# Attention and two MLPs on one core: the first MLP of blocks one to five from float32r to float16 parts

## The chip, the cores and the metric

The kernel runs on one core of a Trainium2 chip. The metric is the device time of one execution in microseconds. A profiled execution gives the span from the first instruction to the last, and the busy times of TensorE (PE, with its weight loads as PEld), VectorE (DVE), ScalarE (ACT), GpSimd (POOL) and the queue that issues DMAs (SP).

## The reference

q, k and v have 4 batches, 8 heads, 576 positions and 64 dimensions; there are 2304 tokens of width 512 and two MLPs with 2048 inner columns, all float32.

```python
scores = scale * np.matmul(q, k.transpose(0, 1, 3, 2))
scores = np.where(block_i >= block_j, scores, -1000000000.0)   # blocks of 64 positions
attn = np.exp(scores - np.max(scores, axis=-1, keepdims=True))
attn = attn / (np.sum(attn, axis=-1, keepdims=True) + 1e-09)
x = np.matmul(attn, v)          # then heads side by side: 2304 x 512
h = x @ moe_w_in
x = np.maximum(0.01 * h, h) @ moe_w_out
h = x @ moe2_w_in
return (h * (1.0 / (1.0 + np.exp(-h)))) @ moe2_w_out
```

## The kernel before

The tokens are worked in six blocks of 384. Attention of block b+1 runs beside the first MLP of block b; the second MLP follows for all tokens at the end, in seven products for each pair (a Strassen scheme).

The weights lie in memory as pairs of 32-bit words (64-bit numbers): `convert` makes float32 of them. `w0`, the sign and the top word of each number are taken from the raw load: ACT scales the top word (L429), ACT or DVE puts the low word's bits in place (L437 to L443), DVE masks the sign (L446), shifts the exponent by 3 (L450, `shifted`) and adds the two (L455, `added`). With `joint` the last two are one instruction, shift and or (L459, `joined`); the second MLP's weights have that form. The first MLP's w1 comes in 32 pieces of 128x512, two for each of 16 inner chunks f (side 0 of the input weight, side 1 of the output weight). Block zero uses them whole in float32, as they arrive.

For blocks one to five each operand is a float32r pair, high and low part, and each product three matmuls (low weight by high x, high by low, high by high). `split_weights` makes w1's parts (high on ACT or DVE at L381 and L383, low on DVE at L392), `take_pair` those of x from PSUM (L1089, L1094), and `g_hi`, `g_lo` those of the gate. `first_layer` (L1611 to L1613) and `second_layer` (L1640) are the matmuls: 4 chunks of 128 rows by 3, 12 each, so 24 of 384 columns in a step (blk, f), 16 steps a block. They are issued in two cuts of six.

Attention of a block has four groups of two heads. For each, `values_of` loads V, takes its largest absolute value (L1023), spreads it and turns it over the partitions by a transposing DMA (L1029), reduces again (L1034), forms a power of two and its inverse from the exponent (L1037 to L1048), and splits V in float16 parts (L1052, L1057). Scores (L1305) are float32r parts, the weights of attention float16 parts, turned by transposing DMAs; `weigh_all` issues their products with V (L1155) into one bank, and `take_pair` scales them back as it takes x out. One staging ring of V holds a single group. x has two sets of tiles, for even and odd blocks: x of block b+1 waits until the first layers of block b-1 are through (`x_free`).

The order of the instructions on every engine is computed before: `Schedule` takes tasks with dependencies, durations and ranks and plays them through; among what is ready the lowest rank goes first. A step's rank is 16 times its block plus f; `GATE`, `SHORT` and `CHAIN` put gates, attention on PE and the maximum of a row ahead of all. The first MLP's and the second's matmuls form one chain (`in_turn`): first layer of a step, then second layer of the step before. Attention of block b has ranks from 16(b-1) + `ATT` on, over 12.8 (`ATT_SLOPE` 0.8 of 16); splits of w1 for step f have 16 + f + 55; conversions 10.5 + 0.7 f.

`SLOTS` divides 32 slots of two 128x512 float32 tiles: w1's parts of chunk f are in slots 2f and 2f+1, the whole w1 in the last 15 to 16 until block zero has used it, and as slots become free in block five the second MLP's operands go there (`emptied`, `place_of`). After the last step of a block four evacuations take its output to staging tiles and memory (`add_second`, `evac`); the second layer of the next block's first step waits for all four, since it uses the same banks.

Of the kernel before, what the change touches and what calls it, by code (L numbers as in the profile page):

```python
# [19 lines left out]
P = 128  # L20
# [13 lines left out]
NATIVE = 15  # L34
# [11 lines left out]
ATT0, ATT1, ATT, ATT_SLOPE, AHEAD, V_LATE = 11.0, 0.3, 60.0, 0.8, 7.5, 0.0  # L46
# [15 lines left out]
SQUARE, RANGE = 2.0**-16, 2.0**-68  # L62

# [178 lines left out]
def attn_mlp_mlp(  # L242
# [56 lines left out]
    SLOTS = {"y": (0, 3), "x": (3, 3), "e": (6, 3), "xw": (9, 2), "t1": (11, 1), "t2": (12, 1), "l": (30, 2)}  # L299
# [24 lines left out]
    def emptied(name):  # L324

        return [steps[base + slot_of(name)[-1] // 2].t_g2]
# [83 lines left out]
    def convert(src, f, sl, rk, load_rank, to=None, slow=0, lag=0, joint=False, free=()):  # L410
# [41 lines left out]
        def added(e):  # L452
            ci = d["c"].bitcast(I32)
            d["x"] = d["c"].bitcast(F32) if to is None else to
            engine[e].tensor_tensor(d["x"].bitcast(I32), d["y"].bitcast(I32), ci, op=ALU.add)  # L455
# [35 lines left out]
    def first_weights():  # L491

        got = []
        for i in range(2 * NF):
            f, sl = i // 2, slice((i % 2) * DM, (i % 2 + 1) * DM)
            rk = CONV0 + CONV1 * f
            to = wx[f][:, sl] if f < NATIVE else None
            got.append(convert(w1, f, sl, rk, LOAD0 + RAW0 + 20 * i if i < 4 else rk - CONV_LOAD, to, slow=LATER if i < 4 else 0))
        return got

    def split_weights():
# [3 lines left out]
        for i in range(2 * NF):  # L505
            f, sl = i // 2, slice((i % 2) * DM, (i % 2 + 1) * DM)
            d, t_x, users = w1_got[i]
# [6 lines left out]
            deps = [t_x]  # L514
            for at in (2 * f, 2 * f + 1):
                j = at - len(spare) - len(kq1)
                if at in slot_of("xw"):
                    deps += [t for u in units for t in (u.t_turn, u.t_pv)]
                elif at < len(spare):
                    deps += x_done[0]  # L520
                elif j < 0:
                    deps += kq1_users
# [24 lines left out]
    def second_places():  # L547
# [8 lines left out]
        place.step = slot_of("xw")[-1] // 2  # L556
        w2_places.append((place, 2 * TWO))
        k = slot_of("t2")[-1] + 1
        while len(w2_places) < 7 * NF // 2 - 2:
            place = Place(lambda t, k=k: slot(k, "r" if t == F32R else "rh", t), ())  # L560
            place.step = k // 2
            w2_places.extend([(place, 0), (place, DM)])
            k += 1
# [4 lines left out]
    def place_of(p, k, halved=False):  # L568
# [7 lines left out]
        if hasattr(place, "step"):  # L576
            deps = y_there[NBLK - 2][:2] if place.step is None else [steps[base + place.step].t_g2]
# [285 lines left out]
    v_ring, vp_ring = ring("v", VR, F32), ring("vp", 2 * VR, F16)  # L863
    v_small = pp.tile([P, 8], F32, tag="vs", name="vs")
# [19 lines left out]
    class Group:  # L884


        def __init__(self):
            self.x, self.evac = None, []
            self.t_turn, self.t_top, self.v_users = None, None, []

    heads, groups, s_users, units = [], [], [], []
# [4 lines left out]
    t_least = plan.add(  # L896
# [3 lines left out]
    def attention(blk):  # L900
# [95 lines left out]
        def values_of(mine, rk):  # L996
            g, k = groups[-1], len(groups) % 2
            last, older = (groups[-2] if len(groups) > 1 else None), (groups[-3] if len(groups) > 2 else None)
            total = sum(words_of_v(two[0][3]) for two in mine)
            g.rs, g.rv = v_ring.take(total), vp_ring.take(2 * total)  # L1000
            stage, both = v_ring.view(g.rs, total), vp_ring.view(g.rv, 2 * total)
            hi, lo = both[:, :total], both[:, total:]
            small = v_small[:, 4 * k : 4 * k + 4]
            most, top, mult, g.back = (small[:, i : i + 1] for i in range(4))
            t_load, g.v, at = [], [], 0
            for two in mine:
                _, b, _, q1, h = two[0]
                nj, n = (q1 + P - 1) // P, words_of_v(q1)

                def load(b=b, h=h, nj=nj, to=stage[:, at : at + n]):  # L1010
                    nc.sync.dma_start(
                        out=to.rearrange("p (h x) -> p h x", h=2),
                        in_=vL[b, h : h + 2, :, :nj, :].rearrange("h p j d -> p h (j d)"),
                    )

                t_load.append(dma(freed(g.rs), rk + 0.5, P * 4 * n, load, lag=V_LAG))
                for i in (0, 1):
                    sl = slice(at + i * n // 2, at + (i + 1) * n // 2)
                    g.v.append([part[:, sl].rearrange("p (j d) -> p j d", d=D) for part in (hi, lo)])
                at += n  # L1020

            def summed(e):
                nc.vector.tensor_reduce(most, stage, axis=AX.X, op=ALU.max, apply_absolute_value=True)  # L1023
# [1236 lines left out]
```

## Time and profile before

| | |
|---|---|
| median of 3 runs | 898.11 us (897.71 to 899.44) |
| profiled execution | 897.39 us, span 895.7 us |
| PE busy | 882.3 us (99%), 6569 matmuls |
| PEld busy | 796.9 us (89%) |
| DVE busy | 775.9 us (87%), 1794 instructions |
| ACT busy | 626.8 us (70%), 1428 instructions |
| granted TensorE clock | 1.000 over the span |
| HBM read and written | 93.85 and 35.65 MB |

Matmuls are pipelined and their ends are modelled, so a busy PE is not PE at its peak; the pitch at which matmuls start says more. Block zero's MLP runs from about 35 to 136 us, block one from 132, block five to 548; the two halves of the second MLP follow. A row of a timeline gives the start, the duration, the engine, the line and operation, and what the instruction writes and reads by the program's names (h, l: parts of x; the w and slot names: weights; s: scores; vs: V's scalars).

### The profile page before, as it was taken

To read this page: it belongs to the slowest core of one execution; us is meant where nothing else is said; L and a number is where in the kernel's file an instruction comes from. 1 tells how busy PE (TensorE), PEld (TensorE's weight loads), DVE (VectorE), ACT (ScalarE), POOL (GpSimd) and SP (SyncE) were. 2 spreads that over 40 slices of the span, in tenths; PEclk is the share of its full clock that TensorE was granted. 3 is DMA by queue.
4 is the path that set the end of the run, shared out by engine and by line. 5 is a ranking of instruction groups with operands and counts; after the bars stand their busy time and mean duration, and the time that the engine had idled before them with its cause. 6 is when DMAs were issued, how large, how long until landed. Compare 5 with 4: busy or idle time off the path is not lost.

```text
span 895.7 us, 18467 instructions
## 1 busy us (share of the span) xinstructions
PE 882.3 (99%) x6569; PEld 796.9 (89%) x6569; DVE 775.9 (87%) x1794; ACT 626.8 (70%) x1428; POOL 17.8 (2%) x81
## 2 busy tenths in 40 slices
PE   9999999999999999999999999999999999999997
PEld 4655569999999999999999998999999988888886
DVE  6898899998889899888755998889887999999986
ACT  7998688776766677777645766979887995444432
POOL 0000000000000000000000000000000000000000
PEclk9999999999999999999999999999999999999999
DMA  7588836766675688866625446687865884554531
GB/s 240 173 234 199 237 110 167 141 144 148 155 156 121 144 187 156 157 170 156 126 45 177 153 159 194 221 289 226 292 229 191 296 263 135 166 152 132 166 106 59
DMA packets 181291, 156.13 MB, mean 174 GB/s; under 512 B 110416, under 2 KB 157264, under 8 KB 181200
## 3 DMA queue, kind: packets, MB, share of 16 engines
q1 hardware_dynamic: 181200, 154.97, 63.4%
q8 instruction: 51, 0.84, 0.4%
q14 instruction: 40, 0.33, 0.1%
HBM read 93.85 MB, written 35.65 MB: 145 GB/s over the span
## 4 chain that ended last, share of the span: by engine, by line
PE 81%; DVE 11%; ACT 4%; DMA 2%; issue 2%; SPq 0%; DVEq 0%; ACTq 0%
PE acc L1640 11%; PE acc L2055 8%; PE s L2055 5%; PE h L1611 5%; PE h L1612 5%; PE h L1613 5%; PE s L1305 4%; PE u L1640 4%; PE h L1606 4%; PE x L1155 3%; PE u L2055 3%; PE x L2055 2%; PE acc L1876 2%; PE acc L1877 2%; PE acc L1632 2%; PE acc L1878 2%
## 5 line engine op out<-in xcount | busy, mean ns | idle before, releaser
L1323 ACT ACTIVATE p<-s,st 128x288 f32<-128x288 f32 (+4 forms) x120 | 62.5, 522 | 46.3 <-DVE st L1315 26.9
L1668 ACT ACTIVATE g<-h 128x384 f32<-128x384 f32 x96 | 46.8, 488 | 49.5 <-PE h L1613 43.2
L1305 PE MATMUL s<-k,q 128*128 128x288 f32 (+5 forms) x288 | 65.8, 324 | 1.2 <-ACT p L1323 1.0
L1640 PE MATMUL acc<-ghi,w 128*128 128x384 f32 x255 | 66.6, 337 | 0.0
L1337 ACT ACTIVATE hl<-p,st 128x576 f16<-128x576 f32 (+5 forms) x91 | 54.9, 622 | 14.1 <-DVE st L1333 5.4
L392 DVE TENSOR_TENSOR glo<-g,ghi 128x384 fp32r<-128x384 f32 x80 | 44.3, 553 | 20.4 <-ACT ghi L381 19.9
L1342 DVE SCALAR_TENSOR_TENSOR hl<-p,st,hl 128x576 f16<-128x576 f32 (+4 forms) x96 | 59.0, 625 | 2.3 <-ACT hl L1337 1.5
L1611 PE MATMUL h<-h,w 128*128 128x384 f32 x180 | 60.7, 337 | 0.0
L2055 PEld LDWEIGHTS <-y 128*128 128x128 f16 x525 | 51.2, 98 | 6.8 <-issue 0.8
L1305 PEld LDWEIGHTS s<-k,q 128*128 128x128 f32 x288 | 47.5, 188 | 7.2 <-ACT p L1323 2.9
L1613 PE MATMUL h<-h,w 128*128 128x384 f32 x160 | 53.6, 335 | 0.0
L1612 PE MATMUL h<-l,w 128*128 128x384 f32 x160 | 53.6, 335 | 0.0
L2055 PEld LDWEIGHTS <-x 128*128 128x128 f16 x492 | 48.1, 98 | 6.0 <-issue 0.5
L1928 ACT ACTIVATE e<-e 128x384 f32<-128x384 f32 (+1 forms) x72 | 42.4, 622 | 9.0 <-DVE e L1908 8.7
L429 ACT ACTIVATE cy<-raw 128x512 f32<-128x512 f32 x64 | 42.8, 669 | 8.3 <-DMA raw<-w 3.9
L1937 ACT ACTIVATE h<-e 128x384 f32<-128x384 f32 x96 | 46.8, 488 | 1.7
L1640 PEld LDWEIGHTS acc<-ghi,w 128*128 128x128 f32 x255 | 45.5, 188 | 0.8
L1640 PE MATMUL acc<-glo,w 128*128 128x384 f32 x120 | 40.2, 335 | 0.0
L381 ACT ACTIVATE ghi<-g 128x384 fp32r<-128x384 f32 x75 | 39.1, 522 | 1.2
L1315 DVE TENSOR_REDUCE st<-s 128x1 f32<-128x320 f32 (+3 forms) x72 | 36.4, 505 | 2.2
L1155 PEld LDWEIGHTS <-vp 128*64 128x64 f16 x1296 | 31.5, 111 | 7.4 <-issue 7.3
L1876 PE MATMUL acc<-h,w 128*128 128x384 f32 x96 | 32.3, 337 | 1.7 <-ACT l L381 1.5
(374 smaller groups left out, 2756.9 us busy)
## 6 DMA issues: line engine op xcount, KB each, us to landing
raw<-w SPq DMA_DIRECT2D x64, 512.0 KB, 4.8
raw<-g SPq DMA_DIRECT2D x64, 256.0 KB, 3.3
g<-e SPq DMA_DIRECT2D x48, 192.0 KB, 3.5
g<-e SPq DMA_DIRECT2D x24, 384.0 KB, 3.4
kqr<-kq_l SPq DMA_DIRECT2D x16, 480.0 KB, 3.9
kqr<-kq_l SPq DMA_DIRECT2D x16, 416.0 KB, 3.8
v<-vL SPq DMA_DIRECT2D x16, 320.0 KB, 3.2
y<-yT SPq DMA_DIRECT2D x12, 384.0 KB, 3.7
```

The lines of the kernel that those rows point to most:

```text
L1155: nc.tensor.matmul(o[i * D : (i + 1) * D, c], v[i][part][:, j], p[i][a], start=start and t == 0, stop=stop and t == len(terms) - 1,)
L1305: nc.tensor.matmul(s[:, :w], hd.q[:, a : a + P], hd.k[:, k0:k1], start=i + j == 0, stop=i == len(hds) - 1 and j == 1,)
L1323: nc.scalar.activation(p[:rows, k0:k1], u.s[piece][:rows, :w], AF.Exp, bias=nm[:rows], accum_out=s2[:rows, piece : piece + 1])
L1337: nc.scalar.activation(hl[:rows, 0, :n], p[:rows], AF.Copy, scale=rc[:rows])
L1342: nc.vector.scalar_tensor_tensor(hl[:rows, 1, :n], p[:rows], rc[:rows], hl[:rows, 0, :n], op0=ALU.mult, op1=ALU.subtract)
L1611: nc.tensor.matmul(h, w1_lo[s.f][:, sl], hi[:, c, : s.n], start=c == 0, stop=False)
L1612: nc.tensor.matmul(h, w1_hi[s.f][:, sl], lo[:, c, : s.n], start=False, stop=False)
L1613: nc.tensor.matmul(h, w1_hi[s.f][:, sl], hi[:, c, : s.n], start=False, stop=c == NC - 1)
L1640: nc.tensor.matmul(s.acc[c][:, : s.n], a, b, start=s.f == 0 and i == 0, stop=s.f == NF - 1 and i == 2)
L1668: nc.scalar.activation(s.g, s.h[:, :n], AF.Prelu, alpha=LEAK)
L1876: nc.tensor.matmul(o, wlo[:, w], xhi[:, x], start=k == 0, stop=False)
L2055: nc.tensor.matmul(o, a[:, x], b, start=i == 0 and j == 0 and q == 0, stop=i == NP - 1 and q == 2, skip_group_check=True,)
```

## The change

Blocks one to five of the first MLP work with float16 parts instead of float32r ones. So that the parts lie in float16's range, both operands are scaled by powers of two. For V there is one factor for a block instead of one for a group: `values_of_all` loads all four groups at once into staging places of their own, takes four maxima and their maximum, and runs the chain with the transposing DMA once; x is taken out of PSUM with a constant scale, and the block's power is put back where its output is evacuated (`y_backs`). For w1 each of the 32 pieces is measured when it is converted (sum of squares on ACT, or largest absolute value on DVE), and the largest over all pieces of a side, turned over the partitions, gives that side's factor; every split then multiplies by it. The gate scales by a constant.

The conversion of w1 takes the form with shift and or (`joint`). The float16 parts of a chunk need one slot instead of two, all 16 whole chunks keep a slot of their own, and the operands of the second MLP's start lie in slots of the whole chunks, which are free long before block five; x's tiles of blocks three and four use the second halves of the float32 areas. Attention's ranks (`ATT`) go from 60 to 54. The output's evacuation of blocks one to four depends on the step's last cut. One pair of second-MLP weights is converted after that MLP's first product.

```diff
-NATIVE = 15
+NATIVE = 16
...
-ATT0, ATT1, ATT, ATT_SLOPE, AHEAD, V_LATE = 11.0, 0.3, 60.0, 0.8, 7.5, 0.0
+ATT0, ATT1, ATT, ATT_SLOPE, AHEAD, V_LATE = 11.0, 0.3, 54.0, 0.8, 7.5, 0.0
...
+W_RANGE, DOWN = 2.0**-66, 2.0**-23
+V_SLOTS = ((16, 17, 18, 19), (20, 21, 25, 26))
+SPLIT_LEAD, W_RANK, VB_LEAD = 55.0, 0.4, 4.0
...
-    SLOTS = {"y": (0, 3), "x": (3, 3), "e": (6, 3), "xw": (9, 2), "t1": (11, 1), "t2": (12, 1), "l": (30, 2)}
+    SLOTS = {"y": (16, 3), "x": (19, 3), "e": (22, 3), "xw": (9, 2), "t1": (25, 1), "t2": (26, 1), "l": (30, 2)}
...
-        return [steps[base + slot_of(name)[-1] // 2].t_g2]
+        return [t for k in slot_of(name) for t in slot_free(k)]
+
+    slot_users = {}
+
+    def slot_free(k):
+
+        if k < NF:
+            return [steps[base + k].t_g2]
+        f = k - NF
+        return [steps[f].t_g2, *w1_done[2 * f], *w1_done[2 * f + 1], *slot_users.get(k, ())]
...
-            to = wx[f][:, sl] if f < NATIVE else None
-            got.append(convert(w1, f, sl, rk, LOAD0 + RAW0 + 20 * i if i < 4 else rk - CONV_LOAD, to, slow=LATER if i < 4 else 0))
+            to = lambda f=f, sl=sl: wx[f][:, sl]
+            got.append(convert(w1, f, sl, rk, LOAD0 + RAW0 + 20 * i if i < 4 else rk - CONV_LOAD, to, slow=LATER if i < 4 else 0, joint=True))
...
+    def measure_weights():
+
+        t_zero = plan.add({"POOL": 150}, [], -100, lambda e: nc.gpsimd.memset(w_sums, V_LEAST))
+        tasks = []
+        for i, (d, t_x, _) in enumerate(w1_got):
+            at = i % 2 * (2 * NF + 1) + i // 2
+
+            def sized(e, d=d, at=at):
+                if e == "ACT":
+                    nc.scalar.activation(
+                        w_junk, d["x"], AF.Square, scale=SQUARE, accum_out=w_sums[:, at : at + 1]
+                    )
+                else:
+                    nc.vector.tensor_reduce(
+                        w_sums[:, at + NF : at + NF + 1], d["x"], axis=AX.X, op=ALU.max, apply_absolute_value=True
+                    )
+
+            tasks.append(plan.add({"ACT": act(DM) + 200, "DVE": dve(DM)}, [t_x, t_zero], CONV0 + CONV1 * (i // 2) + W_RANK, sized))
+        return tasks
...
+        def turned():
+            nc.sync.dma_start_transpose(out=tops, in_=w_wide)
...
+        t = plan.add({"DVE": 190}, measure_weights(), rk, squared)
+        t = plan.add({"DVE": 200}, [t], rk, most)
+        ts = [plan.add({"ACT": act(P), "DVE": 170}, [t], rk, lambda e, s=s: spread(e, s)) for s in (0, 1)]
+        t = dma(ts, -1000.0, 80640, turned, 1200, lag=PT_LAG)
+        t = plan.add({"DVE": dve(2 * P) + 90}, [t], rk, topped)
+        t_half = plan.add({"DVE": 160}, [t], rk, halved)
+        t = plan.add({"DVE": 130}, [t_half], rk, inverted)
+        t_mult = plan.add({"DVE": 130}, [t], rk, ranged)
+        t = plan.add({"DVE": 130}, [t_half], 0, turned_back)
+        w1_range.update(mult=mult, t_mult=t_mult, t_back=plan.add({"DVE": 160}, [t], 0, both_back))
...
-                    hi[f], lo[f] = slot(2 * f), slot(2 * f + 1)
+                    both = slot(f, "r16", F16)
+                    hi[f], lo[f] = both[:, : 2 * DM], both[:, 2 * DM :]
...
+            def high(e, d=d, parts=parts, by=by):
+                if e == "ACT":
+                    nc.scalar.activation(parts()[0], d["x"], AF.Copy, scale=by)
                 else:
-                    deps += [steps[j].t_g2, *done[2 * j], *done[2 * j + 1]]
-            ts = split(DM, lambda d=d: d["x"], parts, deps, step_of(1, f) - LEAD + i % 2, [last] if last else [])
-            last = ts[0]
-            if f >= NATIVE:
-                users += ts
-            done.append(ts)
+                    nc.vector.tensor_scalar(parts()[0], d["x"], by, None, op0=ALU.mult)
+
+            def low(e, d=d, parts=parts, by=by):
+                nc.vector.scalar_tensor_tensor(
+                    parts()[1], d["x"], by, parts()[0], op0=ALU.mult, op1=ALU.subtract
+                )
...
+            deps = [t_x, w1_range["t_mult"]]
+            if f in slot_of("xw"):
+                deps += [t for u in units for t in (u.t_turn, u.t_pv)]
+            elif f < len(spare):
+                deps += x_done[0]
+            else:
+                deps += kq1_users
+            rk = step_of(1, f) + SPLIT_LEAD + side
+            t_hi = plan.add({"ACT": act(DM, False, 1), "DVE": dve2x(DM, 1)}, deps, rk, high, [last] if last else [])
+            t_lo = plan.add({"DVE": dve(DM, 1)}, [t_hi], rk, low)
+            last = t_hi
+            done.append([t_hi, t_lo])
...
-        while len(w2_places) < 7 * NF // 2 - 2:
+        for k in (27, 28, 29, *range(9), *range(11, NF)):
             place = Place(lambda t, k=k: slot(k, "r" if t == F32R else "rh", t), ())
-            place.step = k // 2
+            place.step = k
...
+            at = NC * NB if blk in (3, 4) else 0
             x_hi[blk], x_lo[blk] = (
-                area(f"{s}{blk % 2}", "r", F32R).rearrange("p (c t) -> p c t", c=NC) for s in "hl"
+                area(f"{s}{blk % 2}", "x16", F16)[:, at : at + NC * NB].rearrange("p (c t) -> p c t", c=NC) for s in "hl"
...
+        def values_of_all(pairs, rk):
+
+            k = blk % 2
+            small = v_small[:, 8 * k : 8 * k + 8]
+            mosts, most, top, mult, back = small[:, :4], *(small[:, 4 + i : 5 + i] for i in range(4))
+            before = v_blocks[-1] if v_blocks else None
+            b = Block()
+            v_blocks.append(b)
+            b.mult, b.stages, b.loads, b.splits = mult, [], [], []
+            t_mosts = []
+            for i, mine in enumerate(pairs):
+                total = sum(words_of_v(two[0][3]) for two in mine)
+                if blk == 1:
+                    stage = lambda i=i, n=total: area("l0", "v")[:, i * n : (i + 1) * n]
+                    free = []
+                elif blk == 2:
+                    name = ("h1", "l1", "l0", "h0")[i]
+                    stage = lambda name=name, n=total: area(name, "x16", F16)[:, NC * NB :].bitcast(F32)[:, :n]
+                    free = x_free[2] if i > 1 else []
+                else:
+                    s = V_SLOTS[k][i]
+                    stage = lambda s=s, n=total: slot(s, "v", F32)[:, :n]
+                    free = area_free(s)
...
+                def sized(e, i=i, stage=stage):
+                    nc.vector.tensor_reduce(mosts[:, i : i + 1], stage(), axis=AX.X, op=ALU.max, apply_absolute_value=True)
+
+                old = v_blocks[-3].splits if len(v_blocks) > 2 else []
+                t_mosts.append(plan.add({"DVE": dve(total) + 40}, [*loads, *old], rk + 1, sized))
+                b.stages.append(stage)
+                b.loads.append(loads)
...
+            t_most = plan.add({"DVE": 200}, t_mosts, rk + 1, summed)
+            t_wide = plan.add(
+                {"ACT": act(P), "DVE": 170}, [t_most, before.t_turn if before else None], rk + 1, spread
+            )
+            t_turn = b.t_turn = dma(
+                [t_wide, before.t_top if before else v_least], SHORT + rk, 40320, turned, 1200, raw_done, lag=PT_LAG
+            )
+            t_top = b.t_top = plan.add({"DVE": dve(P) + 90}, [t_turn], rk + 1, topped)
+            t_down = plan.add({"DVE": 130, "POOL": 200}, [t_top], rk + 1, smaller)
+            b.t_mult = plan.add({"DVE": 160}, [t_down], rk + 1, factor)
+            t_pow = plan.add({"DVE": 160}, [t_down], rk + 8, power)
+            b.splits.append(t_pow)
+            b.t_y_back = plan.add({"DVE": 160}, [t_pow, w1_range["t_back"]], rk + 9, y_back)
+            b.splits.append(b.t_y_back)
...
-                    nc.scalar.activation(o, i, AF.Copy, scale=group.back)
+                    nc.scalar.activation(o, i, AF.Copy, scale=1.0 / PS)
...
+            if blk:
+                nc.scalar.activation(s.g, s.h[:, :n], AF.Prelu, alpha=LEAK, scale=DOWN)
...
-            s.ghi = gp.tile([P, NB], F32R, tag="ghi", name="ghi")[:, :n]
+            s.ghi = gp.tile([P, 2 * NB], F16, tag="ghi", name="ghi")[:, :n]
...
-            time = len(cs) * (3 * mm(n) if blk else mm32(n))
+            time = len(cs) * (3 * mm16(n) if blk else mm32(n))
...
+                back = y_backs[:, blk : blk + 1]
+                if not blk:
+                    copy(e, d["y"], s.acc[c][:, :n])
+                elif e == "ACT":
+                    nc.scalar.activation(d["y"], s.acc[c][:, :n], AF.Copy, scale=back)
+                else:
+                    nc.vector.tensor_scalar(d["y"], s.acc[c][:, :n], back, None, op0=ALU.mult)
...
-            t = plan.add(copy_on(n, True), [cut_done[c], *free], GATE + rk, evac, after)
+            time = {"ACT": act(n, True, 1), "DVE": dve_psum(n) + 61} if blk else copy_on(n, True)
+            t = plan.add(time, [cut_done[c] if blk == NBLK - 1 else s.t_g2, *free, *y_scaled], GATE + rk, evac, after)
...
+                if b == i == 0:
+                    first_pair(NP - 1)
...
-                    x_free[blk + 1] = [steps[-2].t_g1]
+                    if blk == 1:
+                        x_free[2] = [steps[NF - 1].t_g1, *v_blocks[0].splits]
+                    elif blk < 4:
+                        x_free[blk + 1] = v_blocks[1].splits
+                    elif blk == 4:
+                        x_free[blk + 1] = [steps[2 * NF - 1].t_g1]
```

Left out are the further operations of the two range chains (spread, maximum, exponent bits), the loads of V and its splits, which keep their form, and declarations.

## Rows read from the trace of the kernel before

**Rows 1.** Timeline of PE, last step of block five: start us, us, operation

```profile
539.16 0.33 PE L1611 MATMUL h<-h,l 128*128 128x384 f32 x1
...
543.32 0.33 PE L1876 MATMUL x<-x,w 128*128 128x384 f32 x1
```

**Rows 2.** Windows: length, busy us (x instructions) of each engine, clock, DMA

```profile
39.00:124.00 85.00, 85.00 (x412) 48.92 (x412) 76.33 (x220) 71.54 (x164) 1.56 (x6) 1.00 0.77 208
123.50:218.90 95.40, 94.58 (x751) 86.03 (x750) 90.10 (x243) 71.34 (x172) 5.00 (x24) 1.00 0.66 139
219.00:308.00 89.00, 88.80 (x769) 85.92 (x767) 76.46 (x230) 59.86 (x157) 2.92 (x12) 1.00 0.63 138
308.00:384.00 76.00, 75.86 (x677) 73.03 (x677) 68.93 (x197) 54.51 (x135) 5.43 (x23) 1.00 0.86 175
384.00:470.00 86.00, 86.00 (x757) 84.47 (x757) 64.86 (x194) 55.02 (x141) 2.09 (x8) 1.00 0.54 118
```

**Rows 3.** Timeline of DVE: last conversion, x's low parts, V's chain

```profile
122.79 0.69 DVE L455 CUSTOM_DVE_ANT_0 cc<-cy,cc 128x1024 uint16<-128x1024 uint16 x1
...
218.31 0.61 DVE L1094 SCALAR_TENSOR_TENSOR l<-x,vs,h 128x384 fp32r<-128x384 f32 x1
...
307.25 0.61 DVE L1094 SCALAR_TENSOR_TENSOR l<-x,vs,h 128x384 fp32r<-128x384 f32 x1
...
383.27 0.61 DVE L1094 SCALAR_TENSOR_TENSOR l<-x,vs,h 128x384 fp32r<-128x384 f32 x1
...
443.14 1.08 DVE L1023 TENSOR_REDUCE vs<-v 128x1 f32<-128x896 f32 x1
...
450.28 0.28 DVE L1034 TENSOR_REDUCE vs<-vt 128x1 f32<-128x130 bf16 x1
```

**Rows 4.** Timeline of PE: first matmul of blocks one to five

```profile
131.73 0.34 PE L1611 MATMUL h<-h,y 128*128 128x384 f32 x1
...
220.42 0.34 PE L1611 MATMUL h<-h,y 128*128 128x384 f32 x1
...
306.85 0.34 PE L1611 MATMUL h<-h,y 128*128 128x384 f32 x1
...
394.24 0.36 PE L1611 MATMUL h<-h,y 128*128 128x384 f32 x1
...
476.76 0.33 PE L1611 MATMUL h<-h,y 128*128 128x384 f32 x1
```

**Rows 5.** Chain in order of time, float16 matmuls of 512 and 256 columns

```profile
16.74 1.73 PE h L1443 x8
...
745.55 1.97 PE acc L2055 x18
```

**Rows 6.** Groups by form, 39 to 124 us: busy us, mean ns | idle before

```profile
L450 DVE TENSOR_SCALAR cy<-cy 128x512 uint32<-128x512 uint32 x27 | 11.0, 417 | 0.5 <-ACT cy L429 0.4
...
L392 DVE TENSOR_TENSOR y<-w,y 128x512 fp32r<-128x512 f32 x2 | 1.4, 686 | 0.0
...
L381 ACT ACTIVATE y<-w 128x512 fp32r<-128x512 f32 x4 | 2.5, 618 | 0.0
```

**Rows 7.** Groups by form, the whole span

```profile
L1937 ACT ACTIVATION_READ_ACCUMULATOR h<-e 128x1 f32 x96 | 18.1, 188 | 0.0
...
L596 DVE SCALAR_TENSOR_TENSOR w<-l,t,w 128x512 f16<-128x512 f32 x18 | 13.1, 745 | 0.6 <-ACT w L591 0.4
...
L687 ACT ACTIVATE h<-l 128x512 f32<-128x512 f32 x16 | 9.6, 600 | 1.1 <-DVE l L459 0.8
```

**Rows 8.** Instructions on V's small scalars: ns min/median/max, first and last start

```profile
L1034 DVE TENSOR_REDUCE vs<-vt x20: 267/278/282, 40.4 to 450.3; 128x1 f32<-128x130 bf16 x20
...
L1045 DVE TENSOR_SCALAR vs<-vs x20: 134/147/155, 41.5 to 450.8; 128x1 int32<-128x1 int32 x20
```

**Rows 9.** Timeline of ACT, evacuation of block four's output

```profile
480.65 0.87 ACT L381 ACTIVATE y<-acc 128x384 f32<-128x384 f32 x2 [0.56 <-PE acc L1640]
```

**Rows 10.** Timeline of PE, border of first and second MLP

```profile
550.20 0.44 PE L1876 MATMUL acc<-h,w 128*128 128x384 f32 x1 [1.51 <-ACT l L381]
```

More of the change, by code (lines that the diff above doesn't have):

```diff
@@ L324, in emptied, with area_free @@
     def emptied(name):
-        return [steps[base + slot_of(name)[-1] // 2].t_g2]
+        return [t for k in slot_of(name) for t in slot_free(k)]
[5 more added lines that the diff above has]
+        return [steps[f].t_g2, *w1_done[2 * f], *w1_done[2 * f + 1], *slot_users.get(k, ())]
+    def area_free(k):
+        first, n = next(a for a in SLOTS.values() if a[0] <= k < a[0] + a[1])
+        got = list(slot_users.get(k, ()))
+        for f in range(first - NF, first - NF + n):
+            got += [steps[f].t_g2, *w1_done[2 * f], *w1_done[2 * f + 1]]
+        return got
     def cc_room(dtype):
@@ L501, in split_weights @@
+    w1_range = {}
     def split_weights():
@@ L576, in place_of @@
         if hasattr(place, "step"):
-            deps = y_there[NBLK - 2][:2] if place.step is None else [steps[base + place.step].t_g2]
+            deps = y_there[NBLK - 2][:2] if place.step is None else slot_free(place.step)
         if halved:
@@ L994, in parted_keys @@
             hd.keys = [hd.rk, hd.rq]
[L996 to L1020, printed above, removed]
@@ new lines, in values_of_all, with load @@
+        def values_of_all(pairs, rk):
[20 more added lines that the diff above has]
+                    free = area_free(s)
+                loads, at = [], 0
+                for two in mine:
+                    _, bt, _, q1, h = two[0]
+                    nj, n = (q1 + P - 1) // P, words_of_v(q1)
+                    def load(bt=bt, h=h, nj=nj, at=at, n=n, stage=stage):
+                        nc.sync.dma_start(
+                            out=stage()[:, at : at + n].rearrange("p (h x) -> p h x", h=2),
+                            in_=vL[bt, h : h + 2, :, :nj, :].rearrange("h p j d -> p h (j d)"),
+                        )
+                    loads.append(dma(free, rk + 0.5, P * 4 * n, load, lag=V_LAG))
+                    at += n
+                def sized(e, i=i, stage=stage):
[4 more added lines that the diff above has]
+                b.loads.append(loads)
@@ L1022, in summed @@
             def summed(e):
[L1023 removed]
+                nc.vector.tensor_reduce(most, mosts, axis=AX.X, op=ALU.max)
             def spread(e):
@@ new lines, in values_of_all, with values_of @@
+            b.t_mult = plan.add({"DVE": 160}, [t_down], rk + 1, factor)
[3 more added lines that the diff above has]
+            b.splits.append(b.t_y_back)
+        def values_of(i, mine, rk):
+            g, b = groups[-1], v_blocks[-1]
+            total = sum(words_of_v(two[0][3]) for two in mine)
+            g.rv = vp_ring.take(2 * total)
+            both = vp_ring.view(g.rv, 2 * total)
+            hi, lo = both[:, :total], both[:, total:]
+            g.v, at, stage = [], 0, b.stages[i]
+            for two in mine:
+                n = words_of_v(two[0][3])
+                for j in (0, 1):
+                    sl = slice(at + j * n // 2, at + (j + 1) * n // 2)
+                    g.v.append([part[:, sl].rearrange("p (j d) -> p j d", d=D) for part in (hi, lo)])
+                at += n
@@ L1099, in take_pair @@
             rk = SHORT + rank_at(done)
-            time = {"ACT": act(n, True, 1), "DVE": dve_psum(n) + 61}
-            t_hi = plan.add(time, [*done_by, group.t_back, *x_free.get(blk, ())], rk, part_hi)
+            time = {"ACT": act(n, True), "DVE": dve_psum(n)}
+            t_hi = plan.add(time, [*done_by, *x_free.get(blk, ())], rk, part_hi)
             t_hi.lag = 0 if blk == 1 else TOP_LAG
-            t_lo = plan.add({"DVE": dve_psum(n) + 61}, [t_hi], rk, part_lo)
+            t_lo = plan.add({"DVE": dve_psum(n)}, [t_hi], rk, part_lo)
             group.evac = [t_hi, t_lo]
@@ L1107, in attention @@
         per_pair = len(todo) // (H // 2)
+        values_of_all(
+            [[todo[k : k + 2] for k in range(i, i + per_pair, 2)] for i in range(0, len(todo), per_pair)],
+            rank_at(-(AHEAD + (VB_LEAD if blk > 1 else 0.0)) * P),
+        )
         for i in range(0, len(todo), per_pair):
@@ L2193, in attn_mlp_mlp @@
     x_operands(0)
-    for i in range(W2_MID, NF // 2):
+    for i in range(W2_MID, NF // 2 - 1):
         first_pair(i)
```

121 lines of the change are left out of this document (71 added, 50 removed).

## Prediction

> **What bounds the kernel now.** The page's busy table came first: PE has nearly the whole span, but since matmul ends are modelled that share proves little. So next came PE's timeline and the chain of waits in order of time. In the last block of the first MLP the 24 matmuls of one step start at 539.16 and are through at 543.32, where the next stage begins [rows 1]: 4.16 us, 173.3 ns each, with no hole. The same regular pitch runs through blocks one to five, with attention's products in between. So PE sets the pace, and its pitch is what the change touches.
>
> Then the windows, one for each stretch [rows 2]. From 39 to 124 us (block zero, weights converted) DVE is busy 76.3 and ACT 71.5 of 85 us. From 123.5 to 218.9 (block one's MLP, attention of block two, splitting of the weights) DVE has 90.1 of 95.4 us: it is nearly as full as PE. Afterwards it falls to 86, 91 and 75%.
>
> How late attention is stands in two timelines. The last low part of block two's x begins at 218.31 and that of block three at 307.25 [rows 3]; PE begins those blocks at 220.42 and 306.85 [rows 4], the third with its first two chunks. Attention arrives just in time there, so a faster PE can overtake it. Block four's x is there near 383.9, its MLP starts at 394.24: 10 us of lead [rows 3, 4].
>
> **Float16 products.** Blocks one to five have 80 steps of 24 matmuls, 1920, all 384 columns wide. A float16 matmul of that width is not in the trace; neighbours are: 18 of 256 columns take 1.97 us (109.4 ns, 106.7 for the columns at 2.4 GHz plus 2.8) and 8 of 512 take 1.73 us (216.3, 213.3 plus 2.9) [rows 5]. Both give 2.8 ns over the columns, against 13.3 for float32r. I take 160 + 2.8 = 162.8 ns, so 10.5 ns saved on each: 0.253 us a step, 4.04 a block, **20.2 us** in all. Bounds: 10.4 to 10.6 ns a matmul, 20.0 to 20.4.
>
> The Trainium skill, "TensorE: Matmul & The Clock Gate", section Back-to-back issue gap, gives N/2.4 + 2.5 ns for an isolated warm matmul. That would be 162.5 ns here and 20.7 us in all; the trace's 2.8 decides.
>
> **Conversion.** 27 of the 32 shifts lie in the first window, 417 ns each, 11.0 us of DVE [rows 6]; they go, and shift and or become one instruction in the place of the addition. Measuring adds 32 instructions: a squared sum as on ACT in the second MLP, 600 + 188 ns [rows 7], or a maximum on DVE (1.08 us for 896 columns [rows 3], so an estimate of 0.65 for 512). That is 25 us on ACT, 21 on DVE. But 16 high halves (4 in the row shown, six such rows; 618 ns), 9.9 us, and five low halves (two in the row shown, 686 ns), 3.4 us [rows 6], can no longer be made before the range is known and leave the window. Net: 21 to 25 added, 24.3 gone, on engines with 22 us free between them [rows 2]. I take 0 for block zero; bounds -1 to +3, since conversion feeds PE closely.
>
> **The range as a gate.** The first split now waits for the maximum over all pieces: last conversion (122.79 + 0.69) [rows 3], 0.8 to measure, three or four small operations, a transposing DMA, four more. The nearest row is V's own chain: its reduction ends at 444.22, the turned row is read at 450.28 [rows 3], 6.1 us, with three 0.15 us operations after it [rows 8]; dropping the shift brings the start forward by about 1. So the factor is there near 130.3, a high half (an estimate of 0.7, from 618 ns without the scale) and a low one (0.745) [rows 6, 7] near 132; PE wants them at 131.73 [rows 4]. Queued behind that first layer in PE's fixed order is the second layer of block zero's last step and all later steps; SP has the transposing load ahead of block two's key loads. I take +1.0; bounds 0 (small operations go at once) and +4 (a DMA slower by the same again, halved by attention filling in).
>
> **Split halves and attention of block two.** The five low halves land in the second stretch (+3.4 us of DVE), 32 low halves cost 745 instead of 686 ns (+1.9) [rows 6, 7], and the range's chain 1.5. V's chain is run once a block instead of four times: 3 x (0.28 + 4 x 0.147) = 2.6 us less a block [rows 8]; x's parts lose the scalar pointer, a little more. Net +4 us in a stretch where DVE is 94% full [rows 2]: x of block two near 218.9 + 4 - 1 = 222, while PE is ready at 220.4 - 4.0 + 1.0 = 217.4. Some of DVE's work there belongs to block three and can wait. I take +3.0; bounds 0 and +7.
>
> **Block three.** Attention needs 89 us for it [rows 2, 3], less 2.6; PE now wants it in 82.4. The rings of x and V staging are deeper, which lets attention run ahead, and DVE has 12 us free [rows 2]. I take +1.5; bounds 0 and +5. Blocks four and five get nothing: attention takes 76 and 86 us there [rows 2], less 2.6 each, and PE 83.3 and 78.5 (between starts [rows 4], less 4.04); block four gains lead, and its 10 us cover the 4.9 that block five loses. Uncovered, 5 us.
>
> **Outputs.** The four evacuations of blocks one to four wait for the step's last cut instead of their own, 6 matmuls, 1.0 us later, and take a scale. Behind them PE's second layer of the next block waits; the cover is the next first layer, 12 x 163 ns = 1.95 us. Two evacuations take 0.87 us on ACT [rows 9], four 1.8 alone, less if DVE shares. +0.7 for four borders; bounds 0 and +2.5.
>
> **Second MLP.** Its x parts and some weight places come free earlier, another place only after step 10 of block five, and one pair is converted later. PE waits 1.51 us at the border now [rows 10]. I take 0; bounds -1.5 and +3. Gates, their halves and the alternate tile layout have the same counts and columns: the same instructions, so nothing, hidden or not.
>
> **Sum.** -20.2 + 0 + 1.0 + 3.0 + 1.5 + 0.7 + 0 = -14.0. The profiled execution took 897.39 us (span 895.7 and 1.7 around it), so 883.4; the median of the runs shown, 898.11, is 0.7 higher, so **884**. All lower bounds: -22.9, 875; all upper ones: -20.0 + 24.5, some 902.
>
> **Rivals.** (a) *The whole gain*: attention runs ahead in its deeper buffers and nothing waits; -20 to -21, 877.5. For it: 9 to 25% of DVE free after 219 us [rows 2]. Against: the just-in-time arrivals [rows 3, 4].
> (b) *Attention becomes the bound*: it keeps its 251 us for blocks three to five [rows 2] while PE would need 244 (from 220.42 to 476.76 [rows 4], less 12.1), and block two is late by 7. Then 7 + 7 + 1 + 1 come back and some 4 remain: 894. For it: DVE's 94%; against: ranks, not need, order some of that work.
> (c) *Slower: splitting falls behind.* Attention's ranks start at 70 instead of 76 for block two and end 12.8 later, while the split of step f stays at 71 + f; DVE may do 6/12.8 of block two's attention before each split that came earlier until now. Of 90 us in the stretch some 63 are attention's (27 low halves of 0.69 and the gates' 16, some 0.55 each, off), so up to 29 us are moved ahead, and PE's steps wait in order: 898 - 20 + 29 + 3 = 910. From 17 us it decides. Against it: attention waits on its own rings and transposes, so it is seldom all ready.
> (d) *The format saves nothing*: 898 + 6 = 904. The row of 109.4 ns speaks against it [rows 5]. The Trainium skill states in the same page, section Weight-path perf modes, that the array takes one element per cell and cycle regardless of element width (it says so of fp8 beside bf16); by that rule alone this rival would hold, and the trace disagrees for float32r: 13.3 ns over its columns against 2.8.
>
> **How the numbers follow.** Forecast (880 to 890): 0.55. (a) below 880: 0.22. (b) 890 to 896: 0.11. No change: 0.03. (c) 0.06, (d) 0.03: 0.09 slower. Faster is 0.55 + 0.22 + 0.11 = 0.88. This kernel's measurement tells 0.2% (1.8 us) from no change. The range of 8 in 10 leaves out half of the slower side, no change and the ends of (a) and (b): 877 to 893.
>
> **What would show it.** The matmuls of L1611 to L1613 and L1640 at a pitch of 163 ns, a step in block five in 3.9 us, end of the first MLP about 14 us earlier. The range's factor near 130; PE idle before block one's first layer by about 1 us, before block two's by about 3. Twenty transposes of V become five. Wrong it would be if PE shows holes inside block one with splits as releaser (c), if block starts wait for x throughout (b), or if the pitch stays at 173 (d).

## The result and the profile after

The changed kernel takes 890.8 us (889.4 to 891.4), the kernel before 898.1 beside it: ratio 0.9914, 95% interval 0.9897 to 0.9931, 7.3 us faster. That lies in the range, 6.8 us above the forecast of 884, and in the bracket of rival (b), 890 to 896, not in that of the forecast, 880 to 890. The profiled execution took 891.37 us, 6.0 less than the one before; the ledger below is made on those two, so 1.3 us of the difference of the medians is not in it.

Timeline of PE after: the first matmul of blocks one to five, the first of block five's last step, and of the last layers; behind it the last layers' start in the kernel before.

```profile
135.23 0.33 PE L1768 MATMUL h<-h,w 128*128 128x384 f16 x1
227.02 0.34 PE L1768 MATMUL h<-h,w 128*128 128x384 f16 x1
309.63 0.34 PE L1768 MATMUL h<-h,w 128*128 128x384 f16 x1
392.59 0.33 PE L1768 MATMUL h<-h,w 128*128 128x384 f16 x1
470.33 0.33 PE L1768 MATMUL h<-h,w 128*128 128x384 f16 x1
528.83 0.33 PE L1768 MATMUL h<-h,w 128*128 128x384 f16 x1
713.75 0.83 PE L2223 MATMUL x<-w,y 128*128 128x256 f16 x6
```

```profile
724.43 0.83 PE L2055 MATMUL x<-w,y 128*128 128x256 f16 x6
```

In block five 15 steps pass from 470.33 to 528.83: 3.90 us a step, 162.5 ns a matmul, against 173.3 [rows 1]. That is 0.26 us a step, 4.16 a block, 20.8 in all. Set against the starts of before [rows 4], a stage's length shows what it gave back, that is, by how much more than float16's share it differs:

| stage | before | after | of it float16 | given back |
|---|---|---|---|---|
| to block one | 131.73 | 135.23 | 0 | 3.5 |
| block one (with attention of block two) | 88.69 | 91.79 | -4.16 | 7.3 |
| block two | 86.43 | 82.61 | -4.16 | 0.3 |
| block three | 87.39 | 82.96 | -4.16 | -0.3 |
| block four | 82.52 | 77.74 | -4.16 | -0.6 |
| block five and second MLP to its last layers | 247.67 | 243.42 | -4.16 | -0.1 |
| last layers to the end of the span | 171.27 | 175.85 | 0 | 4.6 |

20.8 gained and 14.7 given back leave 6.1. Three places hold the loss: the stretch before block one, block one, and the last layers. The holes, in which PE stands still, are in PE's timeline after (in brackets the wait and its releaser, the instruction that ended it):

```profile
123.59 0.56 PE L1462 MATMUL s<-k,q 128*128 128x320 f32 x2 [1.75 <-ACT p L1480]
...
205.51 1.22 PE L1462 MATMUL s<-k,q 128*128 128x512 f32 x2 [1.51 <-ACT p L1480]
207.55 0.50 PE L1768 MATMUL h<-h,w 128*128 128x384 f16 x1 [0.82 <-DVE w L619]
207.84 0.53 PE L1769 MATMUL h<-l,w 128*128 128x384 f16 x1
...
717.27 2.72 PE L2223 MATMUL s<-w,y 128*128 128x256 f16 x12 [2.70 <-DVE e L2069]
719.79 1.01 PE L2223 MATMUL x<-w,x 128*128 128x256 f16 x6
```

In the kernel before, the products that correspond to those at 717.27 follow 1.31 us after the last layers' start:

```profile
725.74 1.47 PE L2055 MATMUL s<-w,y 128*128 128x256 f16 x12 [0.48 <-DVE e L1901]
```

The step at 207.55 is step 13 of block one. Its second product starts 0.29 us later, where 0.16 was due. Windows after (length, busy us of PE, PEld, DVE, ACT, POOL, clock, DMA) show what the engines did:

```profile
39.00:130.00 91.00, 89.02 (x427) 51.33 (x428) 77.96 (x227) 78.18 (x205) 0.76 (x4) 1.00 0.73 194
124.00:227.00 103.00, 98.78 (x776) 61.84 (x774) 97.96 (x255) 84.57 (x195) 5.62 (x24) 0.97 0.67 159
...
200.00:207.50 7.50, 4.13 (x76) 2.68 (x70) 7.10 (x23) 5.81 (x16) 0.41 (x2) 0.82 0.65 145
207.50:211.40 3.90, 3.85 (x13) 1.82 (x14) 3.65 (x7) 0.40 (x2) 0.20 (x1) 0.50 0.72 137
...
717.00:720.00 3.00, 2.73 (x14) 1.87 (x13) 2.73 (x5) 2.97 (x8) 0.00 (x0) 0.50 0.77 271
```

From 200 to 207.5 us PE is busy for 4.13 of 7.5 us. Within them the granted clock falls: in finer windows it is 1.00 up to 203.5 (PE busy for 2.41 of 3.5 us), 0.92 to 205, and 0.50, which is 1.2 GHz instead of 2.4, from 205 to 211.4. Twelve products of step 13 so come at 0.32 us each, 1.9 us lost on top of the waits. The same happens behind the hole at 717. DVE is busy 97.96 of 103 us from 124 to 227, 95%.

DVE's timeline after: last conversion, the turned row of the range, the factor, the first low halves of the weights, step 13's, and the last low part of block two's x:

```profile
119.36 0.69 DVE L479 SCALAR_TENSOR_TENSOR l<-cy,cc 128x512 uint32<-128x512 uint32 x1
...
127.90 0.41 DVE L562 TENSOR_REDUCE wm<-wt 128x2 f32<-128x256 bf16 x1
...
129.42 0.17 DVE L573 TENSOR_SCALAR wm<-wm 128x2 f32<-128x2 f32 x1
...
131.04 2.07 DVE L619 SCALAR_TENSOR_TENSOR w<-y,wm,w 128x512 f16<-128x512 f32 x3
...
206.76 0.73 DVE L619 SCALAR_TENSOR_TENSOR w<-w,wm,w 128x512 f16<-128x512 f32 x1
...
226.90 0.55 DVE L1247 SCALAR_TENSOR_TENSOR l<-x,h 128x384 f16<-128x384 f32 x1
```

The factor is there at 129.6 and the first low half at 131.7; block two's x at 227.4, against 218.9 before [rows 3], and its first matmul stands at 227.02. Conversion in groups by form, 39 to 124 us:

```profile
L457 ACT ACTIVATE cc<-raw 128x512 uint16<-128x512 uint32 x6 | 4.6, 768 | 0.0
...
L530 ACT ACTIVATE wj<-w 128x512 bf16<-128x512 f32 x6 | 3.8, 625 | 1.4 <-DVE w L479 1.3
...
L461 DVE TENSOR_SCALAR cc<-raw 128x512 uint16<-128x512 uint32 x22 | 9.9, 452 | 2.4 <-DMA raw<-w 2.4
...
L1372 DVE MEMSET s<- 64x64 f32 x22 | 2.5, 112 | 5.2 <-PE s L1369 5.1
```

Of the 32 measuring instructions 31 are on ACT (L530). The low words of the conversion, which ACT took before in 22 of 27 cases, are now on DVE in 22 of 28, 9.9 us, nearly what the 27 shifts took, 11.0 [rows 6]. And yet DVE stands idle for 13.0 of the 91 us before 130. In the kernel before it was 8.8, and the low words were on ACT:

```profile
39.00:130.00 91.00, 91.00 (x431) 52.56 (x431) 82.19 (x232) 76.84 (x177) 1.56 (x6) 1.00 0.73 199
...
L439 ACT ACTIVATE cc<-raw 128x512 uint16<-128x512 uint32 x22 | 17.0, 774 | 0.0
```

### The profile page after: what moved, and what is told of

Same layout as the page of the kernel before. It is cut to its first block, busy times and chain, and to the rows that moved or that the text cites. A ratio compares the mean times of both kernels' runs of the same rounds, so it can differ in the third digit from the quotient of the medians.

```text
span 889.6 us, 18360 instructions
## 1 busy us (share of the span) xinstructions
PE 866.6 (97%) x6569; PEld 650.4 (73%) x6569; DVE 765.1 (86%) x1730; ACT 633.7 (71%) x1455; POOL 15.3 (2%) x75
## 4 chain that ended last, share of the span: by engine, by line
PE 68%; DVE 9%; ACT 4%; DMA 2%; issue 2%; SPq 0%; DVEq 0%; POOL 0%; ACTq 0%; POOLq 0%
PE acc L1797 11%; PE acc L2223 7%; PE h L1768 5%; PE h L1770 5%; PE h L1769 5%; PE s L2223 5%; PE s L1462 4%; PE u L1797 4%; PE x L1312 2%; PE u L2223 2%; PE x L2223 2%; PE acc L2045 2%; PE acc L2044 2%; PE acc L2046 2%; PE s L2044 1%
## 5 line engine op out<-in xcount | busy, mean ns | idle before, releaser
L1797 PEld LDWEIGHTS <-w 128*128 128x128 f16 x840 | 78.6, 98 | 54.6 <-issue 4.4
L1797 PE MATMUL acc<-ghi,w 128*128 128x384 f16 x420 | 103.1, 328 | 0.8 <-ACT cc L1901 0.8
L1768 PE MATMUL h<-h,w 128*128 128x384 f16 x280 | 92.6, 331 | 0.8 <-DVE w L619 0.8
L1769 PE MATMUL h<-l,w 128*128 128x384 f16 x280 | 92.1, 329 | 0.0
L1770 PE MATMUL h<-h,w 128*128 128x384 f16 x280 | 92.1, 329 | 0.0
L1462 PE MATMUL s<-k,q 128*128 128x288 f32 (+5 forms) x288 | 77.5, 364 | 5.3 <-ACT p L1480 5.1
L1826 ACT ACTIVATE g<-h 128x384 f32<-128x384 f32 x80 | 39.1, 489 | 48.6 <-PE h L1770 47.9
L412 DVE TENSOR_TENSOR glo<-g,ghi 128x384 f16<-128x384 f32 x80 | 44.3, 554 | 28.9 <-ACT ghi L401 28.0
L1797 PE MATMUL acc<-glo,w 128*128 128x384 f16 x210 | 68.5, 326 | 0.0
L1768 PEld LDWEIGHTS <-w 128*128 128x128 f16 x280 | 27.5, 98 | 21.7 <-issue 3.1
L401 ACT ACTIVATE ghi<-g 128x384 f16<-128x384 f32 x77 | 40.2, 522 | 1.4
L1770 PEld LDWEIGHTS <-w 128*128 128x128 f16 x280 | 27.6, 99 | 18.5 <-issue 0.7
L1769 PEld LDWEIGHTS <-w 128*128 128x128 f16 x280 | 27.7, 99 | 15.4 <-issue 0.7
```

Source lines behind the costliest of these rows:

```text
L412: engine[e].tensor_tensor(lo, x, hi, op=ALU.subtract)
L1462: nc.tensor.matmul(s[:, :w], hd.q[:, a : a + P], hd.k[:, k0:k1], start=i + j == 0, stop=i == len(hds) - 1 and j == 1,)
L1768: nc.tensor.matmul(h, w1_lo[s.f][:, sl], hi[:, c, : s.n], start=c == 0, stop=False)
L1769: nc.tensor.matmul(h, w1_hi[s.f][:, sl], lo[:, c, : s.n], start=False, stop=False)
L1770: nc.tensor.matmul(h, w1_hi[s.f][:, sl], hi[:, c, : s.n], start=False, stop=c == NC - 1)
L1797: nc.tensor.matmul(s.acc[c][:, : s.n], a, b, start=s.f == 0 and i == 0, stop=s.f == NF - 1 and i == 2)
```

## The experiments

**Theories.** *Stacked*: the splits can't start before the factor, measuring fills ACT, so DVE leaves time unused before 130 us and has the splits stacked into the full stretch behind it; attention, which needs DVE, is late from there on. *Order*: DVE merely takes attention's work ahead of the low halves that PE wants next.

**e1: no wait for the factor.**

```diff
-  w1_range.update(mult=mult, t_mult=t_mult, ...)
+  w1_range.update(mult=const, t_mult=t_const, ...)   # const = 2**15, 2**16
```

> The weights are still measured, with all 32 instructions and the chain behind them, but the splits multiply by a constant of the same size as the measured one, so that they need not wait for it (the factor's way back to the outputs is unchanged). Theory 'stacked': the loss in block one comes from the splits starting only at 129.6 us, so that about 12 us of low halves fall into a stretch in which DVE is full; with early splits block two should start 4 to 6 us earlier than its 227.0 and the time be 884 to 887. Rival 'order': the loss comes from DVE taking attention's work before the low halves of the last steps (step 13 waits at 207.55); then early splits change only the first steps and the time stays at 889 to 892.

Measured 888.4 us (ratio to before 0.9889, interval 0.9873 to 0.9906): 2.4 less than the changed kernel. Block two starts at 221.11, 5.9 earlier, as 'stacked' had it; the time fell by less, between the two expectations. Of the 5.9 us 4.3 are left at the start of block five (466.04), and 2.4 in the time.

**e2: no measuring either.**

```diff
-  t = plan.add({"DVE": 190}, measure_weights(), rk, squared)
-  ...
+  nc.gpsimd.memset(mult[:, 0:1], 2.0**15)   # and 2**16, 2**-8
```

> Left out are the 32 measuring instructions and the chain that finds the factor; constants of the same size stand in their place. 'Stacked': as without the gate, and some 25 us of ACT and DVE work before 124 us less, so that the hole of 1.75 us at 121 to 123.6 us goes too: 882 to 885. 'Order': only that hole goes: 888 to 890.

882.7 us (0.9832, 0.9817 to 0.9846), as 'stacked' had it: measuring and its wait cost 8.1 us together, 5.7 of them beyond e1. Block two starts at 219.46, block five at 461.52, 8.8 earlier than in the changed kernel.

**e3 and e4: order alone.**

```diff
-SPLIT_LEAD ... = 55.0          -ATT ... = 54.0
+SPLIT_LEAD ... = 45.0   (e3)   +ATT ... = 60.0   (e4)
```

> The rank of every split is 10 us earlier, all else as changed. 'Order': the holes before step 13 (198 to 207.5 us) close and with them the low clock behind them; 884 to 887. 'Stacked': DVE is full either way, attention gets later by what the splits get earlier, block two starts near 226 as before, and the time is 888 to 892.

> Attention's rank goes back from 54 to 60, its value before the change. 'Order': splits stand relatively further ahead, the hole before step 13 shrinks: 885 to 888. 'Stacked': attention of blocks two to five is later by some us, block two starts at 227 or after: 890 to 895.

891.8 (0.9930, 0.9916 to 0.9945) and 891.3 us (0.9928, 0.9913 to 0.9943): no gain, against 'order' in both. In e3 the hole before step 13 is gone (it starts at 197.75), but PE waits for attention's parts instead, 1.59, 2.16, 1.07 and 0.52 us between 215 and 227, and block two starts as its x comes in: DVE's last low part of x, then PE's first matmul, which needs only the first chunk:

```profile
227.88 0.54 DVE L1247 SCALAR_TENSOR_TENSOR l<-x,h 128x384 f16<-128x384 f32 x1
```

```profile
227.63 0.54 PE L1768 MATMUL h<-h,w 128*128 128x384 f16 x1
```

In e4 step 13 starts at 198.51, PE waits 3.71 us for a key part at 218.5, and block two starts at 223.69, 3.3 us earlier than in the changed kernel; 'stacked' had it at 227 or after, so e4's middle fits neither theory. By block five the gain is gone: in e3 and e4 it starts with its x, at 470.2 and 470.3. 'Order' falls: another order moves the wait and does not shorten the whole.

**e5: less work for PE.**

```diff
-  nc.tensor.matmul(h, w1_lo[s.f][:, sl], hi[:, c, : s.n], ...)
```

> Left out is one of the three products of the first layer in blocks one to five (low weights with high x), 320 matmuls of 163 ns, 52 us of PE work; everything else stays. If PE is the bound in all these blocks the time falls by about 50 us, to near 841. If attention (its DVE, ACT and transposes) is the bound in blocks one to four, only block five's 64 matmuls, 10.4 us, come off surely, and block five starts at 460 to 467 us instead of 470: 872 to 880.

871.0 us (0.9697, 0.9681 to 0.9713): of 52 us taken from PE, 19.8 come off. Block five starts at 457.9, 12.4 earlier, where 256 matmuls, 41.6 us, had gone before it; of block five's own 10.4 us 6.0 show before the last layers. PE's waits from 124 to 458 us (us, times, longest):

```profile
PE s L1462 <- ACT p L1480: 13.1, 20, 1.6
PE s L1462 <- DVE k L412: 9.2, 11, 1.0
```

Attention's softmax and key parts hold PE now. So on the average of these 41.6 us a gain in PE's products is worth about 0.3 of itself in blocks one to four (12.4 / 41.6); what the first few us are worth the run doesn't tell.

**e10: less work for DVE.**

```diff
-  t_lo = plan.add({"DVE": dve(DM, 1)}, [t_hi], rk, low)
```

> Left out are the 32 low halves of the first MLP's weights, 0.74 us of DVE each, 24 us; the matmuls read the high half in their place, so that PE has the same work. If DVE bounds blocks one and two: no hole before step 13, block two starts 8 us or more earlier (by 219), and 8 to 12 us come off: 879 to 883. If the loss lies in latencies, the turns of attention or PE, not in DVE's work: 888 to 891.

885.8 us (0.9858, 0.9842 to 0.9875), between the two expectations: 24 us of DVE less bring 5.0. No hole before step 13 (it starts at 200.28), block two at 221.29. DVE's work is part of the loss, not all: what it does before 124 us stayed as it was.

**e7: half as many measuring instructions.** One factor for both layers.

```diff
-  for i, (d, t_x, _) in enumerate(w1_got):      # 32 pieces of 512 columns
+  for f in range(NF):                           # 16 of 1024, wx[f]
```

> One factor for both layers' weights, measured by 16 instructions of 1024 columns instead of 32 of 512; the wait for it stays. Saves some 5 to 6 us of ACT (16 reads of 0.19 us and as many starts). If the cost of measuring is its work, in proportion: 0.25 of 5.7 us, 889 to 890. If the wait alone matters: 890 to 892, not to be told from the changed kernel.

884.2 us (0.9845, 0.9831 to 0.9860): 6.6 less than the changed kernel, where I expected 0.8 to 1.8. The factor is there at 127.6, 2.0 us earlier; block two starts at 217.54, block five at 463.29. Windows 39 to 130 us of the runs without the wait (e1), without measuring (e2), with one factor (e7), to be set beside the changed kernel's above:

```profile
39.00:130.00 91.00, 91.00 (x432) 52.46 (x433) 82.11 (x232) 85.72 (x219) 1.45 (x4) 1.00 0.79 208
```

```profile
39.00:130.00 91.00, 91.00 (x437) 52.85 (x436) 83.64 (x227) 80.94 (x184) 0.76 (x4) 1.00 0.80 211
```

```profile
39.00:130.00 91.00, 90.99 (x435) 52.75 (x434) 81.31 (x236) 78.03 (x187) 0.76 (x4) 1.00 0.78 211
```

PE has no hole in any of them, and DVE's idle time is 8.9, 7.4 and 9.7 us instead of 13.0. All three are faster, but not in that order: e1's ACT is fuller by 7.5 us than the changed kernel's. How e7's 6.6 us divide between the earlier factor and ACT's freed time isn't settled.

**e9: how much chance is in the order.**

```diff
-W_RANK ... = 0.4
+W_RANK ... = 0.6
```

> The same work as in the changed kernel; only the rank of the measuring instructions is later by 0.2, a fraction of a step, which shuffles the order of a few instructions. It tells how far the order alone moves the time. If the 6.6 us between one factor and two are the cost of the work: 889.5 to 892.5. If a chance order made the hole before step 13: anything from 883 to 893, and a start of block two several us away from 227.

891.3 us (0.9916, 0.9895 to 0.9936). With e3 and e4, three other orders of the same work lie within 1.0 us of the changed kernel, so e7's 6.6 is more than such a shuffle was seen to do.

**e6: measuring on POOL.**

```diff
+  nc.gpsimd.tensor_tensor(w_junk, d["x"], d["x"], op=ALU.mult)
+  nc.gpsimd.tensor_tensor(w_top, w_top, w_junk, op=ALU.add)
```

> The weights are measured on POOL (square, then add to a running sum, 64 instructions, one common factor) instead of on ACT and DVE; the wait for the factor stays. If the 25 us of measuring on ACT and DVE before 124 us are what delays attention, block one's attention ends nearer 118 than 117 plus, block five starts 3 to 5 us earlier and the time is 885 to 888; if POOL is slower than about 1.3 us for one of these instructions the factor comes late and the time rises above 895. If only the wait for the factor matters: 890 to 892.

916.8 us (1.0209, 1.0194 to 1.0224). One addition on POOL takes 1.27 us, the factor comes at 158, and DVE is slow up to then; the 32 instructions of L466 after 160 us take 457 ns each again. Groups of e6, 39 to 150 us, then DVE's line in the changed kernel for the same stretch:

```profile
L531 POOL TENSOR_TENSOR wq<-wq,wj 128x512 bf16<-128x512 bf16 x29 | 36.8, 1267 | 2.2
...
L466 DVE TENSOR_SCALAR cc<-raw 128x512 uint16<-128x512 uint16 x28 | 22.3, 802 | 0.0
```

```profile
L466 DVE TENSOR_SCALAR cc<-raw 128x512 uint16<-128x512 uint16 x28 | 12.6, 452 | 0.0
```

**e12: the conversion alone**, in the kernel before.

```diff
-  got.append(convert(w1, f, sl, rk, ..., to, ...))
+  got.append(convert(w1, f, sl, rk, ..., to, ..., joint=True))
```

> The kernel before with one part of the change alone: the conversion of the first MLP's weights shifts and ors in one instruction, 32 shifts of 0.42 us less on DVE, formats and splits as before. If DVE's work before 124 us is hidden behind PE, as the prediction had it: 897 to 898.5, no change. If it makes attention earlier as leaving out the measuring did: 892 to 896.

899.3 us (1.0006, 0.9997 to 1.0015): no change: the shifts' 11 us of DVE were hidden. In its profiled execution (899.6 us) block one starts at 134.29, 2.6 later than before, with nothing measured and no factor to wait for. How much of the 3.5 us in the ledger's first row comes with the conversion's new form, and how much differs from one execution to the next, isn't settled.

**e8 and e11: the last layers' border.**

```diff
-  lo = plan.add({"DVE": dve(n, 1)}, [hi], rk, low)
+  lo = plan.add({"DVE": dve(n, 1)}, [hi], rk, low, after)   # after e <- s,s
```

> At the border to the last layers, the low halves of the second and third group of operands wait in DVE's order behind the addition that frees the banks s (at 716.27 in the changed kernel). If this order is what holds PE for 2.7 us at 714.4 to 717.3, with the low clock behind it, 2 to 3.5 us come back: 887 to 889. If DVE is full there in any order, nothing: 890 to 892.

> One factor (16 measuring instructions) together with the order at the last layers' border that gave 0.8 us. If the two add: 883.3. If DVE's order there is a matter of chance: 883 to 885.

e8: 890.0 us (0.9912, 0.9897 to 0.9926), not to be told from the changed kernel. PE's hole is still 2.43 us: sums of the next operands took the place of the low halves in DVE's order. e11, with one factor as well: 884.7 us (0.9849, 0.9832 to 0.9866), the same as e7. In the profiled execution of e8 the clock doesn't fall behind the hole:

```profile
716.68 1.47 PE L2225 MATMUL s<-w,y 128*128 128x256 f16 x12 [2.43 <-DVE e L2070]
```

And yet its last layers take 175.98 us, no less than the changed kernel's 175.85. In all twelve runs of the changed kernel and of e1 to e11 they take 175.3 to 176.5 us, whether PE gets there at 695.34 (e5) or at 739.33 (e6), and whether the clock falls or not; in the kernel before and in e12 171.3. So the 4.6 us come neither with PE's earlier arrival nor with the low clock: they come with something that these twelve have in common and the other two have not. One difference stands in DVE's timelines, after and before: the splits of the last layers' weights begin 23.8 us ahead of PE's start on these layers instead of 32.0, and e2, e4 and e5 too have 23.8, e12 32.0.

```profile
689.94 0.75 DVE L700 SCALAR_TENSOR_TENSOR w<-l,t,w 128x512 f16<-128x512 f32 x1 [2.06 <-ACT w L695]
```

```profile
692.42 0.75 DVE L596 SCALAR_TENSOR_TENSOR w<-l,t,w 128x512 f16<-128x512 f32 x1
```

Which part of the change moves them (one pair of weights converted later, or other places for the operands), and whether that is the cause, no run here tests.

## Why the prediction was right in sign and 6.8 us off

**Float16 products: right.** 162.5 ns where I took 162.8; the term is 20.8 instead of 20.2. The Trainium skill's formula for an isolated warm matmul, N/2.4 + 2.5 (TensorE: Matmul & The Clock Gate, Back-to-back issue gap), gives 162.5 ns; the trace agrees with it. Rival (d) is out: the pitch fell. That does not refute the rule of one element per cell and cycle in the Trainium skill (same page, Weight-path perf modes): 160 ns are the columns' in both formats, what differs is the 13.3 ns and 2.5 ns over them, and no run shows where these come from.

**Conversion, 0: mis-sized.** e12 shows that the saving of 11 us of DVE, near half of the 24.3 that I set against measuring, brings nothing by itself. And measuring costs time: between e1 and e2, which differ by it and its chain alone, lie 5.7 us, and with the wait (2.4) it is 8.1; my sum had 1.0 for the gate and, within the 3.0 for block two, five low halves. I had laid the added 25 us into "22 us free" on two engines. How that time was used up I read from the windows, and e1, e2 and e7 fit it without proving it: ACT took nearly all the measuring, DVE took the low words in exchange, and the splits, which had been DVE's and ACT's reserve of work, were locked behind the factor.

**The range as a gate, +1.0: right time, wrong place.** Factor 129.6 (130.3 forecast), first low half 131.7 (132 forecast). PE didn't wait for it: it came at 135.23, and of the 3.5 us a half is the hole of 1.75 us that attention's exponentials made at 123.6; the rest was there before (block zero's step 13 starts at 116.26, 114.62 in the kernel before), and its cause is not shown. e1 puts the wait's whole cost at 2.4 us, and its effect is that block two's attention is late.

**Splits and attention of block two, +3.0: the step that failed by size.** It measured 7.3, just over its bound of 7. x was due at 222 and came at 227.4. I had counted DVE's work (net +4) and not the unused 4 us before 130, nor that PE would starve: 1.9 us of the 7.3 are the low clock after it.

**Block three, +1.5:** 0.3. Blocks four and five gave back nothing, as forecast. **Outputs, +0.7:** one wait of 0.8 us is all that PE has from them between the blocks.

**Second MLP, 0 (-1.5 to +3): failed at another place.** Its start, which I looked at, kept its length (-0.1). Its last layers lost 4.6, above the bound. In this execution that is 2.2 of waiting more than before (717.27 - 713.75 = 3.52, before 1.31), 1.4 of low clock, 0.9 in one more wait at 759.2; where the clock doesn't fall, as in e8, other waits make up for it. I had read no row there, and the cause stays open.

In all, I had 6.2 us come back, and the ledger has 14.7. That the time still lies in the range is due to the range's width, which came from the rivals and not from these terms. Rival (b) gave 890 to 896, and the time is there, with a chance of 0.11. But its place was wrong: from 227 to 470 us PE waits 0.8 us in all, and blocks three to five lost nothing in the changed kernel. That attention is close behind there is what e5 shows. Rival (c)'s mechanism, low halves behind attention's work, did occur at step 13, and e3 showed that it isn't what costs. Twenty transposes of V became five, as said.

## What to carry to other kernels

When an engine is 95% busy in a stage, ask what work can no longer be done in the stage before, and not only what is added. Two engines with some time free each need not make a place for work that feeds them both. When the bound engine is made faster beside another that just keeps up, price the gain by taking work off it (here 12.4 us for 41.6). And read a row of every later border, also where no format changes: the last layers lost 4.6 us here however early PE came.

## What the runs showed of the hardware

A starved PE can lose twice: after 3.5 us with 2.41 busy and 1.5 us with 0.50 busy the granted clock was 0.50 from 205 to 211.4 us, and behind the hole at 714 to 717 again from 717 to 720; in the kernel before it was 1.000 over the span. It need not: in e4 and e8 PE stands still for 2.40 and 2.43 us at the same place, and the clock stays at 1.00 there. The float16 weight load takes half the time of the float32r one; by form, after and before:

```profile
L1768 PEld LDWEIGHTS <-w 128*128 128x128 f16 x280 | 27.5, 98 | 21.7 <-issue 3.1 <-DVE w L619 1.8
```

```profile
L1611 PEld LDWEIGHTS h<-h,w 128*128 128x128 f32 x180 | 33.8, 188 | 0.2
```

And DVE's 512-column operation rose from 452 to 802 ns while POOL squared the weights and added them up (e6), which made POOL no place for this work.
